# Transposes by the DMA crossbar in a transformer block on one core: LayerNorm output, attention output and phi(k)

## The chip, the core and the metric

The kernel runs on one core of a Trainium2 chip. The metric is the device time of one execution in microseconds. A core has a matrix engine (TensorE, PE in the profile), a vector engine (VectorE, DVE), an engine for activations (ScalarE, ACT), a general one (GpSimd, POOL), a queue engine that only issues transfers (SyncE, SP), and 16 DMA engines. SBUF is the on-chip memory of 128 partitions; PSUM is the small memory into which TensorE writes. Each engine works through its own list of instructions in order, and waits on semaphores for the others.

## The reference

```
x = A_x                                             # 2048 tokens x 448
sa, ca, ga, sb, cb, gb = split(silu(c) @ w_mod)     # six vectors of 448
h = layernorm(x) * (1 + ca) + sa
x = x + ga * A(h)
h = layernorm(x) * (1 + cb) + sb
x = x + gb * B(h)

A: q, k, v = h @ wq, h @ wk, h @ wv                 # 16 heads of 28
   for each of 4 segments of 512 tokens, per head:
       p = softmax(q k^T * 28**-0.5 + causal mask);  a_dot = p v
       a_mem = phi(q) M / (phi(q) z + 1e-6)
       o = g * a_mem + (1 - g) * a_dot              # g = sigmoid(beta)
       M += phi(k)^T v;  z += sum(phi(k))           # phi(t) = t + 1 if t > 0 else exp(t)
   return o @ wo
B: return (sigmoid(h @ w_gate) * (h @ w_up)) @ w_down    # 1792 wide
```

Inputs and outputs are bfloat16.

## The kernel before

The 2048 tokens are four segments of 512, and a segment is four tiles of 128 tokens. The 448 features are cut in four chunks of 112 (`KP`, `NK`). The 16 heads stand in four groups of four (`hc`), each head padded to 32 partitions (`HP`), so that four heads fill the 128 partitions of `qT` and `kT`.

A segment passes through these jobs:

- LayerNorm (class `LN`, lines 206 to 224): statistics, reciprocal root on GpSimd, and `norm`, which writes `xn`, a tile of 128 tokens by 448 features.
- `h_chunk` (line 226): TensorE transposes one chunk of the four `xn` tiles into PSUM (`lntr`), and ScalarE (odd chunks) or VectorE (even ones) scales and shifts it into `hT`, features by tokens. It runs for the first LayerNorm (key `("1", s)`) and the second (`("2", s)`).
- `proj_qk`, `proj_v` (lines 267 to 284): the projections; `qT` and `kT` come out transposed, `vt` not.
- `mem_k` (line 289): `kT` is transposed by TensorE into PSUM (`ptk`), and phi is worked out there by ScalarE and VectorE into `pk`; `mem_update` (line 305) multiplies `pk` with `vt` and adds to the memory `M_sb`.
- `logits` and `pv` (lines 325 and 356), one head group at a time: scores, `exp` on ScalarE, masks on GpSimd; then the products with `vt` and, after segment 0, with the memory. VectorE and GpSimd combine both into `ou`.
- `otr` (line 402): TensorE transposes `ou` into PSUM, VectorE copies it to `oT`. `wo_tile` (line 412) multiplies with `wo`, adds to `x_sb` and begins the second LayerNorm.
- `gate_up` (line 425) and `down` (line 441): the feed-forward part.

The order is written out by hand: a manual schedule in which each engine's list follows the order of the calls. The loop over segments and head groups (from line 551) places `logits`, `pv` and `otr`; between them `run_fill` takes jobs from a list, `fill`, until their listed cost reaches a quota. `fill` holds the projections and memory jobs of the next segment, the output projection and the second LayerNorm of the segment before (appended after that segment's last `otr`), and the feed-forward jobs. `blend` weaves the first LayerNorm of the next segment between those jobs. `later(n, fn)` holds a piece back for n jobs, so that VectorE doesn't stand waiting. PSUM has four buffers (`m`) that projections, transposes and products share, and one large one for the scores.

All transfers run on SP's queue in order, but for three early ones on ScalarE's. The program has eight semaphores for them, used in turn (lanes): a transfer waits until the one eight places before it, on either queue, has landed. `wd_sb` is the landing place of `wq` and `wk` at the start and is loaded with `w_down` later.

Of the kernel before, what the change touches and what calls it, by code (L numbers as in the profile page):

```python
# [17 lines left out]
def kernel(  # L18
# [24 lines left out]
    KP, NK = 112, 4  # L43
    assert KP * NK == D and H * Dh == D and L == 512 and TPS == 4 and F == NFC * P
# [62 lines left out]
    wq_sb = wts.tile([KP, NK, H, HP], BF16)  # L107
    wk_sb = wts.tile([KP, NK, H, HP], BF16)
    wv_sb = wts.tile([KP, NK, D], BF16)
    wo_sb = wts.tile([KP, NK, D], BF16)  # L110
    wg_sb = wts.tile([KP, NK, F], BF16)
    wu_sb = wts.tile([KP, NK, F], BF16)
    wd_sb = wts.tile([P, NFC, D], BF16)
    beta_t = const.tile([P, H], BF16)
    wq_st = wd_sb[0:KP, 0:NK, :].rearrange("p k (h d) -> p k h d", d=Dh)
    wk_st = wd_sb[0:KP, NK:2 * NK, :].rearrange("p k (h d) -> p k h d", d=Dh)
    nc.vector.memset(wq_sb[:, :, :, Dh:HP], 0.0)
    nc.vector.memset(wk_sb[:, :, :, Dh:HP], 0.0)
    nc.sync.dma_start(wq_st, A_wq.rearrange("(k p) (h d) -> p k h d", p=KP, d=Dh))
    nc.scalar.dma_start(wk_st, A_wk.rearrange("(k p) (h d) -> p k h d", p=KP, d=Dh))  # L120
    nc.sync.dma_start(wv_sb[:], A_wv.rearrange("(k p) n -> p k n", p=KP))

    def late_loads():
        load_x(nc.sync, TPS, 2 * TPS)
        nc.sync.dma_start(beta_t[:], A_beta.partition_broadcast(P))
        wm[2] = load_wm(nc.sync, 2)
        load_x(nc.sync, 2 * TPS, 3 * TPS)
        nc.sync.dma_start(wo_sb[:], A_wo.rearrange("(k p) n -> p k n", p=KP))
        wm[3] = load_wm(nc.sync, 3)
        load_x(nc.sync, 3 * TPS, 4 * TPS)  # L130
        for w_sb, w_dram in ((wg_sb, B_w_gate), (wu_sb, B_w_up)):
            wv_ = w_dram.rearrange("(k p) n -> p k n", p=KP)
            nc.sync.dma_start(w_sb[:, 0:2, :], wv_[:, 0:2, :])
            nc.sync.dma_start(w_sb[:, 2:4, :], wv_[:, 2:4, :])
        wm[4] = load_wm(nc.sync, 4)
        nc.sync.dma_start(wd_sb[:], B_w_down.rearrange("(fc p) n -> p fc n", p=P))
        wm[5] = load_wm(nc.sync, 5)
# [10 lines left out]
    cols = const.tile([KP, 4, NK], F32)  # L148
# [12 lines left out]
    vt_all = [const.tile([P, TPS, H, HP], BF16, name=f"vt{s}") for s in range(NSEG)]  # L161
# [18 lines left out]
    def mod_cols(jobs):  # L180
        cp = m_f32("cp")
        for j, vi in jobs:
            for kc in range(NK):
                for k in range(NK):
                    nc.tensor.matmul(cp[0:KP, vi * NK + kc:vi * NK + kc + 1], lhsT=wm[j][:, k, kc * KP:(kc + 1) * KP],
                                     rhs=silu[:, k:k + 1], start=(k == 0), stop=(k == NK - 1))
        for j, vi in jobs:
            src = cp[0:KP, vi * NK:(vi + 1) * NK]
            if vi % 2:
                nc.vector.tensor_scalar(cols[:, vi, :], src, 1.0, None, op0=ALU.add)  # L190
            else:
                nc.vector.tensor_copy(cols[:, vi, :], src)
# [10 lines left out]

    class LN:
        def __init__(self, srcs, key):
            self.srcs, n = srcs, len(srcs)
            self.mv = work.tile([P, n, nc.vector.BN_AGGR_DIM], F32, tag=f"mv{n}", bufs=4, name="mv")
            self.rs = work.tile([P, n], F32, tag=f"rs{n}", bufs=4, name="rs")
            self.out = xns_of.setdefault(key, [])
# [6 lines left out]
        def rstd(self):  # L216
            nc.gpsimd.tensor_scalar(self.rs[:], self.mv[:, :, 1], EPS, None, op0=ALU.add)
            nc.gpsimd.tensor_tensor(self.rs[:], self.rs[:], mhalf[:, 0:len(self.srcs)], ALU.pow)

        def norm(self, i):  # L220
            xn = work.tile([P, D], BF16, tag="xn", bufs=8, name="xn")
            nc.vector.tensor_scalar(xn[:], self.srcs[i], self.mv[:, i, 0:1], self.rs[:, i:i + 1],
                                    op0=ALU.subtract, op1=ALU.mult)
            self.out.append(xn)

    def h_chunk(xns, hT, kc, vi, act_kc=(1, 3)):
        pt = m_bf16("lntr")
        for t in range(TPS):
            nc.tensor.transpose(pt[0:KP, t * P:(t + 1) * P], xns[t][:, kc * KP:(kc + 1) * KP], ident[:])  # L229
        if kc in act_kc:  # L230
            nc.scalar.activation(hT[:, kc, :], pt[0:KP, 0:L], AF.Identity, scale=cols[:, vi + 1, kc:kc + 1],  # L231
                                 bias=cols[:, vi, kc:kc + 1])
        else:
            nc.vector.tensor_scalar(hT[:, kc, :], pt[0:KP, 0:L], cols[:, vi + 1, kc:kc + 1],  # L234
                                    cols[:, vi, kc:kc + 1], op0=ALU.mult, op1=ALU.add)

    xns_of, hT_of = {}, {}

    def ln1_jobs(s):
        box = []  # L240

        def first():
            box.append(LN([x_sb[:, s * TPS + t, :] for t in range(TPS)], s))
            box[0].stats(0)
        jobs = [first] + [lambda t=t: box[0].stats(t) for t in range(1, TPS)] + [lambda: box[0].rstd()]
        jobs += [lambda: None] + [lambda t=t: box[0].norm(t) for t in range(TPS)]
# [10 lines left out]
    def new_hT(key):  # L257
        hT_of[key] = pipe.tile([KP, NK, L], BF16, tag="hT", bufs=3, name="hT")
# [30 lines left out]
    def mem_k(s, t):  # L289
        if t == 0:  # L290
            pk_of[s] = pipe.tile([P, TPS, 512], BF16, tag="pk", bufs=1, name="pk")
        ptk = m_bf16("ptk")
# [315 lines left out]
```

The softmax here doesn't subtract the row's maximum and nothing guards it: scores larger than these inputs give would overflow.

## Time and profile before

| | before |
|---|---|
| median of 3 runs | 307.42 us (307.2 to 311.83) |
| the profiled execution: time | 307.21 us |
| the profiled execution: span, first to last instruction | 305.5 us |
| TensorE busy, matmuls | 277.3 us, 2256 |
| VectorE busy | 175.4 us |
| ScalarE busy | 151.5 us |
| GpSimd busy | 99.6 us |
| mean granted TensorE clock | 0.955 |
| transposes on TensorE: `lntr`, `ptk`, `otr` | 128, 48, 64 |

The profile shows one execution. A group line gives the source line, the engine, the operation, output and inputs with their shapes and the count; then busy time and the mean of one; then the idle time of the engine just before them and what ended it. A line of the windows gives, for a stretch of time, each engine's busy time and count, the granted clock (1.00 is full speed), the share of the DMA engines that is busy, and GB/s. A waits line gives who waited for whom: us in total, how often, and the longest. A line of DMA issues gives the count, the size of each, and the median time from issue to landing. Engines overlap, so shares do not add up to the span.

### The profile page before, as it was taken

How to read it: one execution, taken by the hardware profiler on the slowest of the kernel's cores; microseconds unless marked ns; L12 is line 12 of the kernel's file. 1: busy time of each engine (PE TensorE's matmuls, PEld its weight loads, DVE VectorE, ACT ScalarE, POOL GpSimd, SP SyncE). 2: the span in 40 equal slices, each digit the busy share in tenths (PEclk: the TensorE clock that was granted, in tenths of full speed). 3: DMA queues.
4: the chain of work that ended last, by engine and by line, in shares of the span. 5: the costliest groups of instructions: out<-in, count | busy, mean ns of one | idle time of the engine just before them, and what ended most of it. 6: DMA issues, size and time to landing. Idle time of an engine off the chain costs nothing.

```text
span 305.5 us, 5534 instructions
## 1 busy us (share of the span) xinstructions
PE 277.3 (91%) x2256; PEld 142.9 (47%) x2256; DVE 175.4 (57%) x393; ACT 151.5 (50%) x185; POOL 99.6 (33%) x159
## 2 busy tenths in 40 slices
PE   8888599699886979999998999998999998999995
PEld 3534346284543335545455354444644544544452
DVE  3647694863589535466786254779637558333331
ACT  1456658545955365657436467661675320133300
POOL 0336152713697813131543314326233104000000
PEclk9899999958999689999999799999999999999999
DMA  6999101720000000000001000000100000100001
GB/s 163 280 292 294 58 0 32 233 56 0 3 0 2 0 0 3 0 2 0 2 15 47 0 2 0 4 2 12 35 15 2 0 2 9 37 15 2 0 15 45
DMA packets 12472, 12.84 MB, mean 42 GB/s; under 512 B 1184, under 2 KB 11552, under 8 KB 12448
## 3 DMA queue, kind: packets, MB, share of 16 engines
q1 hardware_dynamic: 11248, 11.48, 13.6%
q10 hardware_dynamic: 1200, 1.03, 1.2%
q8 instruction: 17, 0.28, 0.4%
q14 instruction: 7, 0.06, 0.1%
HBM read 10.67 MB, written 1.84 MB: 41 GB/s over the span
## 4 chain that ended last, share of the span: by engine, by line
PE 66%; DVE 16%; ACT 9%; DMA 3%; issue 3%; POOL 2%; SPq 0%; DVEq 0%; ACTq 0%
PE gps L431 16%; PE ups L436 16%; PE dps L444 13%; PE pq L271 7%; ACT pT L341 5%; PE lg L338 4%; PE acc L366 3%; DMA wd_sb<-in_A_wq_dram 3%; DVE st L213 3%; PE pv L282 2%; DVE x_sb L418 2%; DVE pk L300 2%; DVE pqt L349 2%; ACT hT L231 1%; PE otr L408 1%
## 5 line engine op out<-in xcount | busy, mean ns | idle before, releaser
L341 ACT ACTIVATE pT<-lg 128x2048 bf16<-128x2048 f32 (+1 forms) x48 | 76.5, 1594 | 59.9 <-PE lg L338 59.7
L439 DVE SCALAR_TENSOR_TENSOR fT<-tt,ups 128x512 bf16<-128x512 f32 x56 | 38.4, 686 | 58.2 <-PE ups L436 44.6
L353 POOL TENSOR_SCALAR_AFFINE_SELECT pT<-pT 128x512 bf16<-128x512 bf16 x64 | 40.0, 640 | 68.4 <-ACT pT L341 68.2
L431 PE MATMUL gps<-hT,wg_sb 112*128 112x512 bf16 x224 | 60.1, 389 | 2.0 <-DVE hT L234 0.8
L436 PE MATMUL ups<-hT,wu_sb 112*128 112x512 bf16 x224 | 59.2, 388 | 0.0
L433 ACT ACTIVATE tt<-gps 128x512 f32<-128x512 f32 x56 | 32.9, 596 | 40.4 <-PE gps L431 37.6
L444 PE MATMUL dps<-wd_sb,fT 128*128 128x448 bf16 x224 | 44.2, 353 | 2.3 <-DVE t L393 1.3
L436 PEld LDWEIGHTS <-wu_sb 112*128 112x128 bf16 x224 | 22.0, 100 | 28.7 <-issue 3.3
L431 PEld LDWEIGHTS <-wg_sb 112*128 112x128 bf16 x224 | 20.5, 99 | 27.6 <-issue 5.9
L444 PEld LDWEIGHTS <-fT 128*128 128x128 bf16 x224 | 21.3, 98 | 23.4 <-DVE t L393 1.7
L400 POOL TENSOR_TENSOR ou<-t,t 128x448 bf16<-128x448 f32 x12 | 13.8, 1146 | 53.4 <-DVE t L399 53.4
L271 PE MATMUL pq<-hT,wq_sb 112*128 112x512 bf16 x64 | 19.4, 425 | 5.2 <-DVE pk L300 1.9
L448 DVE TENSOR_TENSOR ot<-dps,x_sb 128x448 bf16<-128x448 f32 x16 | 9.9, 621 | 20.0 <-PE dps L444 20.0
L366 PEld LDWEIGHTS <-pT 128*128 128x128 bf16 x640 | 18.4, 96 | 4.7 <-issue 2.2
L213 DVE BATCH_NORM_STATS2 st<-x_sb 128x6 f32<-128x448 bf16 x32 | 19.8, 618 | 1.1 <-DMA x_sb<-in_A_x_dram 0.6
L271 PE MATMUL pq<-hT,wk_sb 112*128 112x512 bf16 x64 | 19.2, 429 | 0.9 <-DVE x_sb L418 0.9
L366 PE MATMUL acc<-vt,pT 128*128 128x29 bf16 x640 | 18.5, 176 | 1.4 <-DVE pk L300 1.4
L338 PE MATMUL lg<-qT,kT 28*128 28x512 bf16 (+3 forms) x256 | 17.8, 311 | 1.5 <-DVE kT L276 0.8
L231 ACT ACTIVATE hT<-lntr,cols 112x512 bf16<-112x512 bf16 x16 | 11.9, 779 | 14.3 <-PE lntr L229 14.3
L276 DVE CAST kT<-pq 128x512 bf16<-128x512 f32 x16 | 10.9, 679 | 9.8 <-PE pq L271 9.8
L229 PE MATMUL lntr<-ident,xn 128*112 128x128 bf16 x128 | 11.7, 230 | 4.6 <-ACT vt L284 1.8
L274 ACT CAST qT<-pq 128x512 bf16<-128x512 f32 x16 | 9.5, 591 | 12.2 <-PE pq L271 12.1
(78 smaller groups left out, 305.5 us busy)
## 6 DMA issues: line engine op xcount, KB each, us to landing
wm<-in_w_mod_dram SPq DMA_DIRECT2D x5, 392.0 KB, 5.2
out_dram<-ot SPq DMA_DIRECT2D x16, 112.0 KB, 1.7
wg_sb<-in_B_w_gate_dram SPq DMA_DIRECT2D x2, 784.0 KB, 12.4
wu_sb<-in_B_w_up_dram SPq DMA_DIRECT2D x2, 784.0 KB, 15.5
wd_sb<-in_B_w_down_dram SPq DMA_DIRECT2D x1, 1568.0 KB, 8.1
x_sb<-in_A_x_dram SPq DMA_DIRECT2D x3, 448.0 KB, 8.8
wm<-in_w_mod_dram ACTq DMA_DIRECT2D x1, 392.0 KB, 6.1
wd_sb<-in_A_wk_dram ACTq DMA_DIRECT2D x1, 392.0 KB, 8.6
```

The lines of the kernel that those rows point to most:

```text
L213: nc.vector.bn_stats(st[:], self.srcs[i])
L231: nc.scalar.activation(hT[:, kc, :], pt[0:KP, 0:L], AF.Identity, scale=cols[:, vi + 1, kc:kc + 1], bias=cols[:, vi, kc:kc + 1])
L271: nc.tensor.matmul(pq[:, 0:L], lhsT=head_cols(w_sb, k, hc), rhs=h[:, k, :], start=(k == 0), stop=(k == NK - 1))
L338: nc.tensor.matmul(lg[:, hs, wid:wid + nq], lhsT=kT[r, hc, kb * P:(kb + 1) * P], rhs=qT[r, hc, kb * P:L], start=True, stop=True, tile_posi ...
L341: nc.scalar.activation(pT[:, :, w0:w0 + wid], lg[:, :, 0:wid], AF.Exp, scale=scale)
L353: nc.gpsimd.affine_select(out=blk, in_=blk, compare_op=ALU.is_ge, fill=0.0, base=0, pattern=[[0, 4], [1, P]], channel_multiplier=-1)
L366: nc.tensor.matmul(accv[:, qb, hs, 0:ME], lhsT=pT[:, hs, c0:c0 + P], rhs=vt[:, kb, hc * 4 + hs, 0:ME], start=(kb == 0), stop=(kb == qb))
L431: nc.tensor.matmul(gp[:, 0:L], lhsT=wg_sb[:, k, fs], rhs=h[:, k, :], start=(k == 0), stop=(k == NK - 1))
L433: nc.scalar.activation(tt[:], gp[:, 0:L], AF.Tanh, scale=0.5)
L436: nc.tensor.matmul(up[:, 0:L], lhsT=wu_sb[:, k, fs], rhs=h[:, k, :], start=(k == 0), stop=(k == NK - 1))
L439: nc.vector.scalar_tensor_tensor(ft[:], tt[:], 1.0, up[:, 0:L], op0=ALU.add, op1=ALU.mult)
L444: nc.tensor.matmul(dp[:, 0:D], lhsT=fT_of[(s, fc)][:, t * P:(t + 1) * P], rhs=wd_sb[:, fc, :], start=(fc == 0), stop=(fc == NFC - 1))
```

## The change

Three of the four places where TensorE transposes now use a DMA from SBUF to SBUF that transposes (`dma_start_transpose`), all issued on SP's queue: the normalized tiles (for the second LayerNorm, and for the first from segment 1 on; segment 0's first LayerNorm keeps TensorE, as `pe_chunk`), the attention output, and phi(k). Each moves 128 partitions by 512 columns. The feature chunks become 128 rows, the last of them half zeros (`LW` is 64), so `xn` is 512 columns wide with zeros behind the 448; `ou` is padded to 32 columns for each head, and the rows of `wo` are spread out to match. Scale and shift are done on `hT` in place, by VectorE alone. phi(k) is worked out on `kT` before the transpose. The weight loads change shape with the chunks, the loads of the feed-forward weights move from SP's queue to ScalarE's, and the jobs are woven in a different order.

```diff
-    wq_sb = wts.tile([KP, NK, H, HP], BF16)
+    wq_sb = wts.tile([P, NK, H, HP], BF16)
...
+    def load_w(eng, dst, w):
+        eng.dma_start(dst[:, 0:3, :], w[0:3 * P, :].rearrange("(k p) n -> p k n", p=P))
+        eng.dma_start(dst[0:LW, 3, :], w[3 * P:D, :])
...
     def late_loads():
...
-        nc.sync.dma_start(wo_sb[:], A_wo.rearrange("(k p) n -> p k n", p=KP))
+        nc.gpsimd.memset(wo_sb[:], 0.0)
+        for hs in range(4):
+            nc.sync.dma_start(wo_sb[HP * hs:HP * hs + Dh, :, :],
+                              A_wo.rearrange("(c h d) n -> h d c n", h=4, d=Dh)[hs])
...
+        nc.gpsimd.memset(wg_sb[LW:P, 3, :], 0.0)
+        nc.gpsimd.memset(wu_sb[LW:P, 3, :], 0.0)
+
+    def ffn_load_jobs():
+        jobs = []
+        for w_sb, w in ((wg_sb, B_w_gate), (wu_sb, B_w_up)):
+            for k in range(0, 3):
+                jobs.append((0, lambda w_sb=w_sb, w=w, k=k: nc.scalar.dma_start(w_sb[:, k, :], w[k * P:(k + 1) * P, :])))
+            jobs.append((0, lambda w_sb=w_sb, w=w: nc.scalar.dma_start(w_sb[0:LW, 3, :], w[3 * P:D, :])))
+        jobs.append((0, lambda: nc.scalar.dma_start(wd_sb[:], B_w_down.rearrange("(fc p) n -> p fc n", p=P))))
+        return jobs
...
+        def norm_t(self, i):
+            self.norm(i)
+            if i == 0:
+                self.h = new_hT(self.key)
+            nc.sync.dma_start_transpose(self.h[:, :, i * P:(i + 1) * P], self.xn[:, i, :])
+
+        def modulate(self, kc, vi):
+            h = self.h[:, kc, :]
+            nc.vector.tensor_scalar(h, h, cols[:, vi + 1, kc:kc + 1], cols[:, vi, kc:kc + 1],
+                                    op0=ALU.mult, op1=ALU.add)
...
-        jobs = [first] + [lambda t=t: box[0].stats(t) for t in range(1, TPS)] + [lambda: box[0].rstd()]
-        jobs += [lambda: None] + [lambda t=t: box[0].norm(t) for t in range(TPS)]
+        nop = lambda: None
+        jobs = [first] + [lambda t=t: box[0].stats(t) for t in range(1, TPS)]
+        jobs += [lambda: box[0].rstd(0, TPS), nop] + [lambda t=t: box[0].norm_t(t) for t in range(TPS)]
+        jobs += [nop, nop, nop] + [lambda kc=kc: box[0].modulate(kc, 0) for kc in range(NK)]
...
-        ptk = m_bf16("ptk")
-        for hc in range(NHC):
-            nc.tensor.transpose(ptk[:, hc * P:(hc + 1) * P], kT_of[s][:, hc, t * P:(t + 1) * P], ident[:])
-        ek = work.tile([P, 512], BF16, tag="e", bufs=3)
-        nc.scalar.activation(ek[:], ptk[:, 0:512], AF.Exp)
...
+    def mem_k(s, hc):
+        if hc == 0:
+            pk_of[s] = pipe.tile([P, NHC, TPS, P], BF16, tag="pk", bufs=1, name="pk")
+        pkt = work.tile([P, L], BF16, tag="pqt", bufs=3, name="pkt")
+        pk = pk_of[s]
+        phi(kT_of[s][:, hc, :], pkt[:], 2, lambda: nc.sync.dma_start_transpose(pk[:, hc, :, :], pkt[:]))
...
-        op = m_bf16("otr")
-        for t in range(TPS):
-            nc.tensor.transpose(op[0:KP, t * P:(t + 1) * P], ou[:, t, :, :].rearrange("p h d -> p (h d)"), ident[:])
-        nc.vector.tensor_copy(oT_of[s][:, hc, :], op[0:KP, 0:L])
+        nc.sync.dma_start_transpose(oT_of[s][:, hc, :, :], ou[:].rearrange("p t h e -> p (t h e)"))
...
-        ln = LN([xt], ("2", s))
-        ln.stats(0)
-        ln.rstd()
-        later(2, lambda: ln.norm(0))
+        ln.stats(t)
+        ln.rstd(t, t + 1)
+        later(2, lambda: ln.norm_t(t))
...
     def prep_b1():
         ga = mod_rep(2, 1.0, "ga")
+        wm[4] = load_wm(nc.sync, 4)
...
-    fill.extend(blend(j0[7:9] + late + j0[9:], ln1_jobs(1), 2))
-    j1 = j1[:5] + m[0][0:2] + j1[5:7] + m[0][2:4] + j1[7:9] + m[0][4:] + j1[9:] + [(1000, prep_b1)]
-    fill.extend(blend(j1, ln1_jobs(2), 5))
-    j2 = j2[:5] + m[1][0:2] + j2[5:7] + m[1][2:4] + j2[7:9] + [(2000, prep_b2)] + m[1][4:] + j2[9:]
-    fill.extend(blend(j2, ln1_jobs(3), 5))
-    fill.append((1000, prep_b3))
-    fill.extend(j3[:5] + m[2][0:2] + j3[5:7] + m[2][2:4] + j3[7:9] + m[2][4:] + j3[9:])
+    fill.extend(blend(blend(j0[2:4] + [(0, late_consts)] + j0[4:] + m[0][0:4], ln1_jobs(1), 1), ffn_load_jobs(), 3, 2))
+    fill.extend(blend(j1[:6] + m[0][4:] + j1[6:] + m[1][0:4] + [(1000, prep_b1)], ln1_jobs(2)))
+    fill.extend(blend(j2[:6] + m[1][4:] + [(2000, prep_b2)] + j2[6:] + m[2][0:4] + [(1000, prep_b3)], ln1_jobs(3)))
+    fill.extend(j3[:6] + m[2][4:] + j3[6:])
```

The jobs of transposes, of phi(k) and of modulation now have a listed cost of 0 in `fill`. The new `phi` helper does for k what `logits` did for q: `exp` on ScalarE, and a minimum and a combining instruction on VectorE, held back two jobs.

## The prediction

> **What bounds the kernel now.** I read the busy table first, then the time slices, then the stages in windows, then TensorE's waits, then the groups and the DMA issues.
>
> ```profile
> PE 277.3 (91%) x2256; PEld 142.9 (47%) x2256; DVE 175.4 (57%) x393; ACT 151.5 (50%) x185; POOL 99.6 (33%) x159
> PEclk9899999958999689999999799999999999999999
> ```
>
> TensorE is the only engine near full, so work taken off it should shorten the span. But the average hides stages, and the clock row falls to 5, 6 and 7 in single slices. The windows cut the span at four events: the first query projection (13.5), the first projections of segment 1 (33.5), the first output projection (90.8) and the first gate projection (111.8).
>
> ```profile
> 13.50:33.50 20.00, 16.41 (x100) 7.30 (x99) 10.71 (x24) 14.27 (x20) 8.33 (x20) 0.94 0.99 270
> 33.50:90.80 57.30, 49.16 (x510) 29.20 (x509) 37.84 (x83) 35.78 (x49) 27.33 (x35) 0.91 0.16 44
> 90.80:111.80 21.00, 16.25 (x128) 7.94 (x127) 14.30 (x33) 11.91 (x14) 14.01 (x20) 0.83 0.00 1
> 111.80:305.50 193.70, 184.62 (x1452) 92.45 (x1452) 105.92 (x233) 86.29 (x101) 46.89 (x74) 0.98 0.03 11
> ```
>
> The columns are TensorE, weight loads, VectorE, ScalarE and GpSimd, then the granted clock and the DMA share. The last stage is TensorE at 95% and full clock. The three before are 77 to 86% busy with the clock at 0.83 to 0.94: there TensorE waits for others, and after a wait it runs slowly (62.0 to 70.7 us stand at a clock of 0.50 throughout). The waits of 27 to 112 us say for whom:
>
> ```profile
> PE pq L271 <- DVE pk L300: 1.9, 2, 1.6
> ...
> PE lntr L229 <- ACT vt L284: 1.8, 2, 1.4
> PE pq L271 <- ACT hT L231: 1.6, 2, 1.3
> PE acc L366 <- DVE pk L300: 1.4, 1, 1.4
> ```
>
> Most end in results of the three transposes (`pk`, `hT`) that the change moves.
>
> **What leaves TensorE.** 112 of 128 `lntr`, all 48 `ptk`, all 64 `otr`.
>
> ```profile
> L229 PE MATMUL lntr<-ident,xn 128*112 128x128 bf16 x128 | 11.7, 230 | 4.6 <-ACT vt L284 1.8 <-DVE xn L222 0.9 <-DVE t L399 0.8
> ...
> L408 PE MATMUL otr<-ident,ou 128*112 128x128 bf16 x64 | 6.3, 220 | 0.7 <-ACT qT L274 0.7
> ...
> L294 PE MATMUL ptk<-ident,kT 128*128 128x128 bf16 x48 | 4.2, 219 | 1.9 <-DVE ou L390 1.0 <-DVE pk L300 0.6 <-ACT qT L274 0.2
> ```
>
> Busy time includes each batch's drain under the next one, so I price from start to next start in the timeline: four `lntr` 30.26 to 30.53 (68 ns each), eight `ptk` 30.53 to 30.97 (55 ns), four `otr` 45.09 to 45.41 (80 ns). That is 7.6 + 2.6 + 5.1 = 15.3 us of TensorE in all. ScalarE loses 14 evictions of 0.78 us (L231), VectorE 14 of 0.54 (L234) and 16 of 0.42 (L409); it gains 28 in-place modulations, priced at the normalization's 0.42 us (L222: same operation, SBUF to SBUF, 448 columns). TensorE's other matmuls keep their count and width; 128 rows in place of 112 change nothing, since L436 (112 rows, 512 columns) and L510 (128 rows) both step by 0.21 to 0.22 us at full clock.
>
> **What comes in: 56 DMA transposes of 128x512, all on SP's queue.** No row shows one. Let T be the time from the source's last write to landing. Lower bound: the nearest row by size, direction and quiet rings, the output stores, at 1.7 us; upper bound: a 448 KB load among others, 8.8 us.
>
> ```profile
> out_dram<-ot SPq DMA_DIRECT2D x16, 112.0 KB, 1.7
> ...
> x_sb<-in_A_x_dram SPq DMA_DIRECT2D x3, 448.0 KB, 8.8
> ...
> x_sb<-in_A_x_dram SPq DMA_DIRECT2D x1, 224.0 KB, 4.8
> ```
>
> I stay near the store: 1.7 x 128/112 = 1.9, plus half a microsecond to issue (SP's loads: 0.3 to 0.8), so T = 2.5 us in quiet rings. Up to 34 us the rings are full (DMA share 0.99), and I take the 224 KB row's 4.5.
>
> The store row prices a copy, not a transpose. The Trainium skill (VectorE: DVE Perf Modes, The three transpose paths) gives 1309 ns for a 128x128 block through the DMA crossbar against 390 ns on TensorE, and advises TensorE where PSUM will do. If four blocks followed one another, T would be about 5.2 us, an estimate from that page, and the sum below would end near 303.
>
> **Stage by stage.**
>
> 0 to 13.5: nothing. The first LayerNorm keeps TensorE's transposes. The weight loads become pairs, and SP waits for earlier landings between them; the chain was `wq`'s landing at 11.7, and less is queued ahead of it. Gain or loss under 1 us.
>
> 13.5 to 33.5: a loss of 5. Three memsets of 1792 columns now run on GpSimd before its first mask, by `bmask` (464 columns, 0.80 us) about 3.1 us each, from 11.6 to 20.9, where the mask began at 20.07: everything behind moves 0.9. Segment 1's last `xn` ended at 29.2; now 30.1, plus T = 4.5 gives 34.6. VectorE is then held in order at the first modulation, and two `phi` pairs (0.29 + 0.75) stand between the four modulations: 4 x 0.42 + 2 x 1.04 = 3.8, so 38.4 where the last chunk was consumed at 33.1. Nothing covers it but one block of logits. ScalarE meanwhile issues nine weight loads (0.5 us each by its own rows), and the ninth, `wd`, waits for the first transpose on its semaphore lane; behind it stand the last `vt` eviction and the `phi` exponentials, which wait for the same hand-over. If TensorE did not wait there, this would cost about 3 us by itself.
>
> 33.5 to 111.8: a gain of 11. Removed here: 32 `lntr`, 40 `ptk`, 16 `otr`: 2.2 + 2.2 + 1.3 = 5.7. The waits on `pk` and around `ptk` and `lntr` total about 6; I take half, 3, since `phi` stays on ScalarE and VectorE. The slow clock of 62.0 to 70.7 cost 4.3; it follows 2.9 us of idle that `pk` made; half, 2. Segments 2 and 3 have three value projections and `rp`, `acc`, `lg` (5 us) between the last normalization and the first use, so T + 0.42 is hidden; their cover fails from T of about 4.5. The attention transposes start as soon as `ou` is written, some 6 us ahead of the output projection. Then the order changes: four `pq` and one `pv` that stood behind the first output projection now stand ahead of it (+4.3 there, -4.3 behind). Behind it, 21.0 us become the chain: evacuation 0.7, VectorE's list from the first residual add to the last normalization 11.3 (91.5 to 102.8, as now), T = 2.5, four modulations 1.7: 16.2, against 7.7 of matmuls that cover it. Sum: -5.7 - 3 - 2 + 4.3 - 4.8 = -11.2.
>
> 111.8 to 305.5: a gain of 4. Removed: 48 `lntr` (3.3), 44 `otr` (3.5), waits of `lntr` on `t` and of `gps` on `hT` (1.8). Against it: at the last three hand-overs the transposes have 8 to 14 us of down projections over them, but the modulations stand on VectorE behind the last output add: 0.62 + 4 x 0.42, less 0.3 of logits and TensorE's own pace, 1.5 each. -8.6 + 4.5 = -4.1.
>
> Sum: 305.5 + 5 - 11.2 - 4.1 = 295.2 us of span. The profiled execution took 307.21, 1.7 more than its span, and the median is 0.2 above that: 297 us.
>
> **Rivals.**
> - Early stages give nothing (A). For it: VectorE is 66% and ScalarE 62% busy from 33.5 to 90.8, and `phi`, exponentials and casts stay; the waits may only change names. Against it: the waits end in `pk` and `hT`. Then stages two to four return only what the order returns, about 5 for the 5 lost, and the last stage's 4.1 is offset by the ScalarE delay of 3: 306.
> - T is long (B), the one that ends slower. One transpose holds SP's queue until it is nearly done, and every one behind it is late. Price: each us of T above 2.5 costs 1 at the first gate hand-over and, above 4.5, 1 at segments 1, 2 and 3 each; above 6 also 1 at three output projections. T = 6 gives 297 + 3.5 + 4.5 = 305, T = 7.2 is 2% slower, 8.8 gives about 325. For it: four transposes come 0.4 to 0.8 us apart in segment 1. Against it: the store row, and 128 KB is little beside the 270 GB/s of the first stages.
> - All hidden (C): T is 1.9, the first stage loses 2 in place of 5, and the whole slow clock and all waits on `pk` come back: 297 - 3 - 5 = 289.
> - That the transposes are not moved can be excluded: the built program has 56 on SP's queue and 224 matmuls fewer on TensorE.
>
> **How the numbers follow.** Forecast 0.55 (own range 290 to 302), A 0.22, B 0.15, C 0.08. Faster by over 2%, below 301.3, which is about what a measurement of this kernel can tell from no change: 0.52 of the forecast and C, 0.60. Within 2%: A and the forecast's edge, 0.25. Slower: 0.15, B beyond 7.2. The range runs from just under C (286) to 310, B at T of about 6.7; what lies above is most of B, below little.
>
> **What would show it.** In the profile after: transposes landing 2 to 3 us after issue; a TensorE gap of some 8 us around 30 to 38; no stretch at clock 0.5 near 62 to 70; first gate projection at about 106 to 107; the last stage 4 us shorter. The forecast is wrong if SP's queue shows transposes waiting for one another, if the gap before the first gate projection exceeds 12 us, or if TensorE's idle time in 33 to 111 stays as it was.

## The result, and the profile after

The changed kernel takes 323.74 us (median of 4 runs, 322.88 to 324.93), the kernel before 309.52 beside it (307.2 to 311.83): a ratio of 1.049 with a 95% interval of 1.037 to 1.060. It is slower. Ratios are of the means of undisturbed executions: a few executions (one of the four of before here, two of the four of e11 below) ran in a slower state, at a lower clock, and are left out of the ratios. The forecast was 297, with a range of 286 to 310; it missed by 27 us. The profiled execution took 324.38 us, with a span of 322.4.

The busy table and the clock row of the page of the changed kernel:

```profile
PE 267.0 (83%) x2032; PEld 126.3 (39%) x2032; DVE 184.2 (57%) x403; ACT 141.7 (44%) x171; POOL 105.9 (33%) x162
PEclk9969657989999957999679799999968999999999
```

TensorE has 224 matmuls and 10 us of busy time less, as meant. But its share fell from 91 to 83%, and single slices of the clock row still stand at 5, 6 and 7, now far into the last stage too. The windows say where. They are cut at the same events in both kernels: the first query projection, the end of segment 1's first projection, the first gate projection, and the end of the run. (The 33.5 us of the prediction is the end of that projection, not its beginning, as the lines of before further down show.)

```profile
18.20:48.20 30.00, 15.34 (x72) 5.53 (x71) 14.95 (x35) 12.12 (x19) 7.67 (x19) 0.73 0.85 221
48.20:117.30 69.10, 53.73 (x529) 26.99 (x526) 49.17 (x106) 41.72 (x51) 39.36 (x51) 0.92 0.30 62
117.30:322.40 205.10, 186.66 (x1364) 87.99 (x1364) 107.68 (x232) 83.80 (x96) 50.87 (x79) 0.93 0.10 25
```

Against before (13.5, then 20.0, 78.3 and 193.7 us), with what was forecast for each:

| stage | before, us | after, us | change | forecast |
|---|---|---|---|---|
| to the first query projection | 13.5 | 18.2 | +4.7 | 0 |
| to the end of segment 1's first projection | 20.0 | 30.0 | +10.0 | +5 |
| to the first gate | 78.3 | 69.1 | -9.2 | -11.2 |
| to the end | 193.7 | 205.1 | +11.4 | -4.1 |
| span | 305.5 | 322.4 | +16.9 | -10.3 |

In the last stage TensorE has 88 matmuls fewer (1364 for 1452) and is busy 2 us longer (186.66 for 184.62): the clock fell from 0.98 to 0.93. The rest is waiting, and TensorE's waits over the whole span name one producer above all, the in-place modulation of transposed LayerNorm output (line L261):

```profile
PE pq L312 <- DVE hT L261: 18.8, 8, 11.8
PE gps L471 <- DVE hT L261: 14.1, 8, 5.3
PE lg L383 <- ACT pT L386: 4.2, 3, 2.0
```

The columns are microseconds in all, times, and the longest. Most landings are as fast as assumed. The DMA issues, with the median from issue to landing last:

```profile
hT<-xn SPq DMA_TRANSPOSE x28, 2.3
...
oT<-ou SPq DMA_TRANSPOSE x16, 2.4
...
pk<-pkt SPq DMA_TRANSPOSE x12, 2.5
```

T was forecast at 2.5 us in quiet rings, and there the time of one transpose is not what was wrong. At segment 1's hand-over, beside weight loads, it was. First before, where TensorE has three of the four matmuls of that projection done early and waits 1.3 us for the last:

```profile
30.97 0.81 PE L271 MATMUL pq<-hT,wq_sb 112*128 112x512 bf16 x3
33.08 0.38 PE L271 MATMUL pq<-hT,wq_sb 112*128 112x512 bf16 x1 [1.30 <-ACT hT L231]
```

The same place in the changed kernel; the last line is the time from issue to landing of these four transposes:

```profile
32.59 1.61 DVE L250 TENSOR_SCALAR xn<-x_sb,mv,rs 128x448 bf16<-128x448 bf16 x4 [1.99 <-POOL rs L247]
33.32 5.36 SPq L257 DMA_TRANSPOSE hT<-xn  x4
43.78 0.41 DVE L261 TENSOR_SCALAR hT<-hT,cols 128x512 bf16<-128x512 bf16 x1 [2.65 <-DMA hT<-xn]
44.25 0.61 PE L312 MATMUL pq<-hT,wq_sb 128*128 128x512 bf16 x1 [11.76 <-DVE hT L261]
...
47.15 1.01 PE L312 MATMUL pq<-hT,wq_sb 128*128 128x512 bf16 x2 [0.93 <-DVE hT L261]
DMA to landing us min/median/max: 2.5/3.4/6.2
```

The last tile was written at 34.2 and VectorE could begin at 43.8: by the prediction's own definition (from the source's last write to landing) T was 9.5 us there.

### The profile page after: what moved, and what is told of

Its sections match the earlier page's. It is cut to its first block, busy times and chain, and to the rows that moved or that the text cites. A ratio compares the mean times of both kernels' runs of the same rounds, so it can differ in the third digit from the quotient of the medians.

```text
span 322.4 us, 5232 instructions
## 1 busy us (share of the span) xinstructions
PE 267.0 (83%) x2032; PEld 126.3 (39%) x2032; DVE 184.2 (57%) x403; ACT 141.7 (44%) x171; POOL 105.9 (33%) x162
## 4 chain that ended last, share of the span: by engine, by line
PE 52%; DVE 23%; DMA 9%; ACT 6%; POOL 5%; issue 3%; SPq 1%; POOLq 0%; ACTq 0%; DVEq 0%
PE gps L471 14%; PE ups L476 14%; PE dps L484 11%; ACT pT L386 5%; DMA hT<-xn 5%; PE pq L312 4%; DVE xn L250 4%; DVE hT L261 3%; PE acc L405 3%; DVE st L242 3%; PE lg L383 3%; PE pwo L453 3%; DMA pk<-pkt 2%; DVE e L335 2%; DVE pkt L336 2%
## 5 line engine op out<-in xcount | busy, mean ns | idle before, releaser
L471 PE MATMUL gps<-hT,wg_sb 128*128 128x512 bf16 x224 | 63.5, 400 | 14.9 <-DVE hT L261 14.1
L476 PE MATMUL ups<-hT,wu_sb 128*128 128x512 bf16 x224 | 60.3, 393 | 0.0
L471 PEld LDWEIGHTS <-wg_sb 128*128 128x128 bf16 x224 | 20.8, 100 | 43.9 <-issue 17.1
L312 PE MATMUL pq<-hT,wq_sb 128*128 128x512 bf16 x64 | 20.8, 437 | 18.8 <-DVE hT L261 18.8
L476 PEld LDWEIGHTS <-wu_sb 128*128 128x128 bf16 x224 | 22.5, 101 | 29.8 <-issue 5.4
L261 DVE TENSOR_SCALAR hT<-hT,cols 128x512 bf16<-128x512 bf16 x28 | 14.5, 564 | 12.6 <-DMA hT<-xn 12.6
L250 DVE TENSOR_SCALAR xn<-x_sb,mv,rs 128x448 bf16<-128x448 bf16 x32 | 16.8, 545 | 6.5 <-POOL rs L247 6.5
L312 PE MATMUL pq<-hT,wk_sb 128*128 128x512 bf16 x64 | 19.3, 430 | 0.9 <-DVE kT L317 0.9
L541 POOL TENSOR_TENSOR wd_sb<-wd_sb,gb 128x448 bf16<-128x448 bf16 x14 | 15.4, 1111 | 6.4 <-ACT gb L225 6.4
L453 PE MATMUL pwo<-wo_sb,oT 128*128 128x448 bf16 x64 | 16.1, 409 | 0.9 <-DMA oT<-ou 0.8
```

Of the source, the lines that this page charges most:

```text
L250: nc.vector.tensor_scalar(self.xn[:, i, 0:D], self.srcs[i], self.mv[:, i, 0:1], self.rs[:, i:i + 1], op0=ALU.subtract, op1=ALU.mult)
L312: nc.tensor.matmul(pq[:, 0:L], lhsT=head_cols(w_sb, k, hc), rhs=h[:, k, :], start=(k == 0), stop=(k == NK - 1))
L471: nc.tensor.matmul(gp[:, 0:L], lhsT=wg_sb[:, k, fs], rhs=h[:, k, :], start=(k == 0), stop=(k == NK - 1))
L476: nc.tensor.matmul(up[:, 0:L], lhsT=wu_sb[:, k, fs], rhs=h[:, k, :], start=(k == 0), stop=(k == NK - 1))
```

## Experiments

Theory 1 was that the transposes on the crossbar expose idle time at every LayerNorm hand-over, and a slow TensorE clock behind it. Theory 2 was that the edits beside them cost (memsets on GpSimd, weight loads on ScalarE's queue, listed costs of 0, the new order of jobs). Ratios are to the kernel before, run beside each; its median lay between 307.4 and 309.5 us on these occasions, so small steps between kernels that did not run side by side are uncertain by about 2 us. Windows, waits and timelines are of one execution each.

**e1: the memsets run early.**

```
+    nc.gpsimd.memset(wo_sb[:], 0.0)             # behind mhalf's memset
+    nc.gpsimd.memset(wg_sb[LW:P, 3, :], 0.0)
+    nc.gpsimd.memset(wu_sb[LW:P, 3, :], 0.0)
-    ... the same three in late_loads()
```

> Edit: the three GpSimd memsets (padding of the output projection, the gate and the up weights) run before the first LayerNorm instead of beside it. Everything else is as in the changed kernel. Theory 2 (side edits): the memsets share something with VectorE; with them gone from 11.6 to 16.6 us the first four normalizations (L250) fall from 4.5 back to about 1.8 us in all, the first projection starts near 13.6 instead of 18.2, and the whole is 4 to 5 us shorter, near 319. Rival: the slow normalizations have another cause (the transposes' buffers, the wider rows), the start stays at 18 and the time at 324.

Measured: 320.77 us, ratio 1.043 (1.036 to 1.050), and the first projection at 14.3 us. The timeline of the changed kernel, GpSimd first, then VectorE (start, duration, then engine, line and tiles):

```profile
11.61 1.71 POOL L137 MEMSET wo_sb<- 128x1792 bf16 x1
13.38 1.60 POOL L143 MEMSET wg_sb<- 64x1792 bf16 x1
14.92 1.72 POOL L144 MEMSET wu_sb<- 64x1792 bf16 x1
...
10.63 4.47 DVE L250 TENSOR_SCALAR xn<-x_sb,mv,rs 128x448 bf16<-128x448 bf16 x4 [1.49 <-POOL rs L247]
```

and VectorE's same four normalizations with the memsets out of the way (e1):

```profile
10.84 1.77 DVE L250 TENSOR_SCALAR xn<-x_sb,mv,rs 128x448 bf16<-128x448 bf16 x4 [1.57 <-POOL rs L247]
```

4.47 us against 1.77, with nothing changed but what GpSimd does meanwhile. The longest of the normalizations takes 1.74 us, about one memset. So the start is settled: 3.9 of the 4.7 us come back there, and 3.0 reach the end by the medians (the intervals overlap). From e4 to e5 below, the same edit is worth 4.4 us by the ratios. All later kernels with "early memsets" have this edit.

**e2, e3, e4: loads back on SyncE; LayerNorm on TensorE; everything on TensorE.**

```
e2:  -  nc.scalar.dma_start(w_sb[:, k, :], ...), nc.scalar.dma_start(wd_sb[:], ...)
     +  nc.sync.dma_start(...), in late_loads() and, for wd_sb, in prep_b1()
e3:  -  ln.norm_t(t) ... [(0, ... modulate(kc, 2))]
     +  ln.norm(t)   ... [(4 * TR, ... pe_chunk(kc, 2))], and the same in ln1_jobs()
e4:  e3, and phi(k) and otr() as in the kernel before (16 transposes and 4 in PSUM)
```

> Edit: the gate and up weights are loaded on SyncE's queue behind the last rows of x, and the down weights on SyncE in front of the fifth modulation matrix, as the kernel before had them; ScalarE issues no load inside the stages. The transposes stay on the crossbar. Theory 2 (side edits): the 11.8 us that TensorE waits near 32 to 44 us are made by loads that fill the rings while the transposes are under way, and by ScalarE's queue standing 5 us at the down weights; the gap falls to about 6 (four transposes of 1.2 us in a row and 2.3 us of landing), and the time by 6 to 8 us to about 317. Theory 1 (the transposes themselves): the gap stays over 10 us and the time falls by less than 2.

> Edit: the 128 transposes of LayerNorm output go back to TensorE (four to a PSUM tile, the modulation in the eviction, half of it on ScalarE), with the cost that the planner had for them before; phi(k) and attention output stay on the crossbar. Theory 1 (the transposes themselves): every hand-over behind a LayerNorm shortens; the gaps of 11.8, 3.8, 2.9, 6.2 us and those of the second halves go, less 8.7 us of transposes (128 at 68 ns) that TensorE does again, and the time falls by 15 to 20 us, to about 306. Theory 2 (side edits): most of the loss stays, since loads, memsets and job order are unchanged: 318 to 324.

> Edit: all three groups of transposes (LayerNorm output, phi(k), attention output) go back to TensorE; what is left of the change is the 128-row chunks with padding, the memsets, the loads on ScalarE's queue and the new order of jobs. Theory 1 (the transposes themselves): the rest costs about the 4.7 us of the start, so near 311; above the LayerNorm-only variant if the crossbar pays for phi(k) and attention output, below it if it does not: 96 transposes less are 5.7 us (32 at 80 ns and 64 at 55 ns are 6.1). Theory 2 (side edits): 320 or more, the transposes off TensorE being worth what they were forecast to be and the rest eating it.

Measured: e2 323.76 us, ratio 1.051 (1.043 to 1.058); e3 309.98, 1.006 (1.002 to 1.011); e4 309.39, 1.001 (0.996 to 1.005).

In e2 the gate and up weights load earlier and the down weights later. The four transposes of segment 1 land faster, and the 11.8 us wait falls to 7.7:

```profile
DMA to landing us min/median/max: 2.3/2.4/2.4
40.23 0.61 PE L314 MATMUL pq<-hT,wq_sb 128*128 128x512 bf16 x1 [7.66 <-DVE hT L263]
```

So some 4 us of that wait are the loads beside the transposes. But the whole gained nothing: the 1568 KB load then ran beside segment 1's phi(k) transposes, and TensorE waited 4.4 us for them at 77 us. Neither theory had that. e3 says that the LayerNorm transposes hold most of the loss (some 14 us of it), as theory 1 had it. e4 says that the side edits together cost nothing, although the memsets among them cost 3. So something among them had to be a gain.

**e5 and e6: all on TensorE with early memsets; attention output alone on the crossbar.**

```
e5:  e4 with the memsets of e1
e6:  e5, but otr() keeps  nc.sync.dma_start_transpose(oT_of[s][:, hc, :, :], ...)
```

> Edit: all three groups of transposes on TensorE (309.4 us as measured) and the three GpSimd memsets moved ahead of the first LayerNorm. What remains of the change is the 128-row chunks, the loads and the job order. Theory 2 (side edits hold one loss, the memset clash, and one gain, the new order of jobs): the start falls from 18.5 to 14.5 us and the whole by 3 to 4 us, to about 305.5, faster than the kernel before. Rival: the start is given back at the first hand-over to segment 1, and the time stays at 309.

> Edit: as the previous kernel (memsets early, LayerNorm and phi(k) transposes on TensorE), but the attention output goes through the crossbar: 64 transposes off TensorE (5.1 us by the forecast's 80 ns each), and off VectorE the 16 copies out of PSUM. Theory 1: the crossbar costs where its landing is waited for; here two blocks of work lie between issue and use in most blocks, so 3 to 5 us less than the all-TensorE kernel with early memsets, about 301 to 302. Rival: what is gained is lost again at the output projections (waits of 0.8 to 1.7 us each, seen twice) and through longer busy queues: equal to it within 1 us.

Measured: e5 303.36 us, ratio 0.986 (0.978 to 0.995); e6 301.41, 0.980 (0.973 to 0.986). What remains of the change without any DMA transpose (128-row chunks, loads, a new order of jobs; not separated further) is worth 1.4%, about 4 us. The attention output by DMA is worth about 2 more by the medians (the intervals overlap), where 64 transposes had been priced at 5.1 us. Both kernels beat the kernel before.

**e7: matmuls that nobody reads, in the gaps.**

```
+    def idle_mm(n):
+        dm = m_f32("dmy")
+        for _ in range(n):
+            nc.tensor.matmul(dm[:], lhsT=ident[:], rhs=..., start=True, stop=True)   # 512 columns
     h2_jobs:   + [(0, lambda: idle_mm(16 if s < 3 else 1))]
     proj_jobs: + [(0, lambda: idle_mm(32 if s == 1 else 12))]   # segments 1 to 3
```

> Edit: the changed kernel with matmuls of 512 columns whose result nobody reads, placed on TensorE in front of the first gate projections of segments 0 to 2 (16 each) and of the first projections of segments 1 (32), 2 and 3 (12 each): 104 in all, 22 us of work at full clock, into gaps where TensorE waits for landed and modulated LayerNorm output. Theory 1a (most of the loss is the half clock after the gaps, not the gaps): the clock rises from 0.91 to 0.95 or more and the time falls by 5 to 9 us although 104 matmuls are added. Theory 1b (the gaps themselves): the clock behind a gap does not matter, the time is unchanged, or up to 5 us longer where the added matmuls overrun a gap.

Measured: 320.63 us, ratio 1.040 (1.028 to 1.051); the clock rose from 0.91 to 0.95. About 22 us of useless work were added and the kernel became 3 us shorter by the medians (the intervals overlap). Its last stage in the windows:

```profile
118.50:316.20 197.70, 185.40 (x1398) 89.34 (x1396) 106.87 (x232) 83.72 (x96) 48.92 (x77) 0.98 0.10 26
```

197.7 us instead of 205.1, with 34 matmuls more. They do not make the modulated rows earlier: at the first hand-over of this stage the gate's first four matmuls end 5.6 us behind the logits ahead of them (177.4 to 183.1 in the changed kernel), and 5.7 here (174.4 to 180.1). What they change is the clock, 0.98 in this stage instead of 0.93. So a gap costs its own length and then a stretch at half clock.

**e8: the listed costs as before.**

```
-    [(0, ... modulate(kc, 2))]   [(0, ... mem_k(s, hc))]
+    [(4 * TR, ...)]              [(4 * TR, ...)]          # and ln1_jobs' modulations
```

> Edit: the changed kernel, where the planner's listed cost of a modulation and of a phi(k) job is 240 again and not 0, so that each softmax block takes the quota of filling work that it had before. No instruction is added or removed, only their order. Theory 2 (the filling work runs out before the second segment's last blocks): the three logits in a row and the 4.2 us that TensorE waits for the exponentials vanish, and 3 to 4 us with them, to about 320. Rival: the quota is not what empties the list; unchanged at 324 within 1 us.

Measured: 320.62 us, ratio 1.043 (1.035 to 1.050). The last stage shortened to 196.3 us and TensorE's waits for exponentials from 4.2 to 2.2, but the first gate moved from 117.3 to 122.3. It is 3 us less than the changed kernel, with intervals that overlap: order matters, but this was a shift more than a cure.

**e9 and e10: where the modulations run, and when.** Both start from e1.

```
e9:   if kc % 2: nc.scalar.activation(h, h, AF.Identity, scale=..., bias=...)
      else:      nc.vector.tensor_scalar(h, h, ...)
e10:  - fill.extend(down_jobs(s - 2)); fill.extend(h2_jobs(s - 1) + gu_jobs(s - 1))
      + dn = down_jobs(s - 2) if s >= 2 else []
      + fill.extend(dn[:3] + h2_jobs(s - 1) + dn[3:] + gu_jobs(s - 1))
```

> Edit: as the changed kernel with early memsets (320.8 us as measured), all transposes on the crossbar, but of the four modulations at a hand-over the odd ones run on ScalarE, as half of the evictions did before. Theory 1c (one engine in order is the cost): at the first gate projection four modulations take 3.5 us in a row on VectorE behind the landing; split, each hand-over shortens by 1 to 1.5 us, so 4 to 7 us over six. Rival: what counts is the landing and the first modulation, and ScalarE's are longer and stand behind exponentials; the time stays within 2 us.

> Edit: as the changed kernel with early memsets (320.8 us), but the modulations of segments 1 and 2 are put in front of the last of the four down projections that fill the hand-over, not behind it. Theory 1d (the landing is long past there, only VectorE's order is late): the waits of 3.5 and 3.3 us for the modulated rows in the last stage go, with the half clock of some 5 to 10 us behind each, and the time falls by 5 to 9 us. Rival: the landed rows themselves are late; at most 1 us.

Measured: e9 315.68 us, ratio 1.026 (1.019 to 1.033), 5 less than e1. e10 309.06, ratio 1.003 (0.999 to 1.008), 12 less than e1, from the place of four modulations in two segments. This hand-over in the changed kernel, SyncE's queue, then VectorE, then TensorE:

```profile
164.34 4.57 SPq L257 DMA_TRANSPOSE hT<-xn  x3
...
169.63 1.19 SPq L257 DMA_TRANSPOSE hT<-xn  x1
...
177.55 0.62 DVE L488 TENSOR_TENSOR ot<-dps,x_sb 128x448 bf16<-128x448 f32 x1 [2.35 <-PE dps L484]
178.09 0.40 DVE L261 TENSOR_SCALAR hT<-hT,cols 128x512 bf16<-128x512 bf16 x1
180.38 0.29 DVE L335 TENSOR_SCALAR e<-e 128x512 bf16<-128x512 bf16 x1 [1.88 <-ACT e L332]
180.71 0.69 DVE L336 SCALAR_TENSOR_TENSOR pqt<-qT,e 128x512 bf16<-128x512 bf16 x1
181.32 1.05 DVE L261 TENSOR_SCALAR hT<-hT,cols 128x512 bf16<-128x512 bf16 x3
...
181.78 1.30 PE L471 MATMUL gps<-hT,wg_sb 128*128 128x512 bf16 x3 [2.85 <-DVE hT L261]
```

The issue of the last transpose began at 169.63, and the landing takes 2.3 us from there: the rows were there at about 172. VectorE idled 2.35 us before 177.55 with that work ready, because in its order the last output add stood in front, and that waited for the last down projection. After one modulation the order put a phi(q) pair in front of the other three, and that waited 1.88 us for ScalarE. TensorE stood meanwhile. The same place in e10, VectorE and then TensorE:

```profile
173.11 2.05 DVE L261 TENSOR_SCALAR hT<-hT,cols 128x512 bf16<-128x512 bf16 x4
175.54 0.62 DVE L488 TENSOR_TENSOR ot<-dps,x_sb 128x448 bf16<-128x448 f32 x1 [0.38 <-PE dps L484]
...
175.77 1.04 PE L471 MATMUL gps<-hT,wg_sb 128*128 128x512 bf16 x4
```

No wait is left, and e10's last stage takes 193.9 us where e1's takes 205.2. The same 1364 matmuls are busy 182.1 us in e10 and 186.7 in the changed kernel: some 4.5 of the 11 us are clock, the rest idle time.

**e11 and e12: which LayerNorm.**

```
e11:  e1, second LayerNorm (wo_tile, h2_jobs) by norm() and pe_chunk()
e12:  e1, both by norm() and pe_chunk()
```

> Edit: early memsets, and of the LayerNorm transposes only the second LayerNorm's (in front of the gate projections) go back to TensorE; the first LayerNorm's (in front of the projections) stay on the crossbar, as do phi(k) and attention output. Read with the next kernel it splits the cost of the LayerNorm transposes. Theory 1: the second LayerNorm holds most, since its chain runs from the output projection to the gate without other work between; 11 to 13 us go, so 308 to 310. Rival: the gap of 11 us at segment 1's projections is the larger part: over 314.

> Edit: early memsets, all LayerNorm transposes on TensorE, phi(k) and attention output on the crossbar. Against the kernel with the attention output alone on the crossbar (301.4 us) this prices phi(k) by DMA; against the changed kernel with early memsets (320.8) all of LayerNorm by DMA. Theory 1: phi(k) is wanted one segment late and hides: 300 to 303. Rival: phi(k) costs, since four of its transposes hold the queue for 5 to 8 us while attention outputs stand behind them: 304 to 307.

Measured: e11 314.86 us (median of 310.81, 313.89, 315.83 and 317.78; no interval), e12 304.84, ratio 0.990 (0.984 to 0.996). With e6 and e1 this is a ladder, each step with one group more on the crossbar; for e11 it has the mean of the first two executions:

| on the crossbar, early memsets | us | step |
|---|---|---|
| nothing (e5) | 303.4 | |
| attention output (e6) | 301.4 | -2.0 |
| and phi(k) (e12) | 304.8 | +3.4 |
| and first LayerNorm (e11) | 312.4 | +7.5 |
| and second LayerNorm (e1) | 320.8 | +8.4 |

phi(k) costs: e12 has a wait that is not in e6.

```profile
PE dM L355 <- DMA pk<-pkt: 5.0, 3, 2.8
```

The two LayerNorms cost about the same. Which costs more is not shown, since the two executions of e11 are 3 us apart; the 11 to 13 us expected of the second did not come. And the second one's step hangs on the order: with the modulations of e10 in place, the crossbar (309.1) is no longer behind TensorE (310.8 and 313.9) for it; the profiled last stages take 193.9 and 197.1 us.

**e13, e14, e15: the first LayerNorm.** All start from e10.

```
e13:  m[s][0:4] (the phi(k) jobs) from behind segment s's jobs to behind j{s+1}[:2]
e14:  e13, wd_sb's load by SyncE in prep_b2() instead of ScalarE in segment 0
e15:  e13, run_fill((quota if s else 0.8 * quota) + debt)
```

> Edit: early memsets, modulations ahead of the last down projection (309.1 us as measured), and the four phi(k) jobs of each segment moved behind the modulations and the first two projections of the next one, so that nothing of phi(k) stands in front of a modulation on VectorE. Order theory: in the kernel it starts from, the modulations of segment 1 are done at 45.2 us, of which 4.4 is one phi(k) product waiting for a free buffer and some 5 are waits and work for its exponentials; the gaps of 10.9 + 0.6 + 4.4 us shrink to 6 to 8 in all and the time falls by 7 to 10 us, to about 300. Landing theory: the four transposes and the full rings set the gap; less than 3 us.

> Edit: as the kernel before in this list, and the 1568 KB load of the down weights moves from ScalarE's queue in segment 0 to SyncE's queue behind the sixth modulation matrix, some 50 us later. Collision theory: the transposes of segment 1 land in 2.5 us instead of 4 to 6, ScalarE does not stand 5 us behind a semaphore lane; 2 to 4 us less than the kernel before in this list. Rival: the collision moves with the load, to the transposes that run beside it at 85 to 95 us; no change or 1 to 3 us longer.

> Edit: as the first kernel of this list, and segment 0's softmax blocks take 0.8 of the quota of filling work, so that more projections are left when the first output projection is reached and stand between it and the first gate. Cover theory: the first gate's gap of 5.3 us closes, with the half clock behind it; 3 to 6 us less than the first kernel. Rival: segment 0's blocks then lack filling work and wait for their exponentials instead; within 1 us or longer.

Measured: e13 321.04 us, ratio 1.040 (1.031 to 1.049); e14 319.15, 1.035 (1.028 to 1.042); e15 318.19, 1.031 (1.022 to 1.040). All are some 8 to 11 us slower than e10 by the ratios.

The reading of the hand-over was right in part. In e10, ScalarE (first line) and VectorE stand like this:

```profile
35.33 0.53 ACT L325 CAST vt<-pv 128x448 bf16<-128x448 f32 x1 [5.09 <-DMA hT<-xn]
...
36.42 0.29 DVE L335 TENSOR_SCALAR e<-e 128x512 bf16<-128x512 bf16 x1 [6.89 <-ACT e L332]
...
43.87 0.69 DVE L336 SCALAR_TENSOR_TENSOR pkt<-kT,e 128x512 bf16<-128x512 bf16 x1 [3.71 <-DMA pk<-pkt]
44.48 0.73 DVE L261 TENSOR_SCALAR hT<-hT,cols 128x512 bf16<-128x512 bf16 x2
```

ScalarE's eviction stands behind the load of the down weights, which waits for a transpose; the exponentials behind it are late; VectorE waits for them with modulations queued behind; and the fourth phi(k) waits until a transpose frees a buffer, with the last two modulations behind it. In e13 the three gaps of 10.9, 0.6 and 4.35 us became one of 8.7, close to the expected 6 to 8. What is left of it is the landing:

```profile
36.08 1.38 DVE L261 TENSOR_SCALAR hT<-hT,cols 128x512 bf16<-128x512 bf16 x4 [6.50 <-DMA hT<-xn]
```

But the phi(k) transposes now had too little work over them, and the wait came back under another name (e13, 44 to 110 us):

```profile
PE dM L356 <- DMA pk<-pkt: 11.5, 7, 2.4
```

with the clock at 0.66 to 0.87 in the windows from 30 to 90 us. The first gate came at 124.9 instead of 115.0. In e14 the DMA share from 30 to 45 us fell from 0.76 to 0.30, and the gap stayed (9.4 us): the load of the down weights is not what makes it. That does not clear the loads as a whole: beside the gate and up weights the four transposes still landed 4.0 to 6.0 us after issue, where e2's took 2.3 to 2.4. In e15 the first gate's gap shrank from 5.3 to 3.8, but an attention output written at 88.5 us was transposed only at 102.1, since SyncE's queue had four phi(k) transposes in front that waited for their sources; the output projection waited 10.7 us for it.

**e16: on the crossbar only what has cover.**

```
e6 with e10's order, and of the second LayerNorm:
+    later(2, lambda: (ln.norm_t if s in (1, 2) else ln.norm)(t))
+    if s in (1, 2): return [(0, ... modulate(kc, 2))]
```

> Edit: early memsets; on the crossbar only attention output and the second LayerNorm of segments 1 and 2 (modulated ahead of the last down projection); phi(k), the first LayerNorms and the second of segments 0 and 3 on TensorE. By the account so far the crossbar pays where other matmuls lie between landing and use: 301.4 us less 32 transposes at 68 ns (2.2 us) and a little clock, 297 to 300. If the gain seen from the order of the modulations was only the undoing of a self-made wait, no better than 301.4.

Measured: 300.75 us, ratio 0.974 (0.965 to 0.982). It beats both kernels and stands beside e6 (0.973 to 0.986): the profiled last stage is 4 us shorter (189.0 for 193.4), but the medians do not tell the two apart.

## Why the prediction was wrong

By size, the miss of 27 us is the last stage (15.5), segment 1's hand-over (5.0), the start (4.7) and the way to the first gate (2.0).

- **The last stage: forecast -4.1, measured +11.4.** The place was right: "the modulations stand on VectorE behind the last output add". The term was mis-sized: 1.5 us for each of three hand-overs. By e1 and e10, two of them cost 11.7 us together. The working counted the add and four modulations. It left out what else stands on VectorE there (at the first hand-over the phi(q) pair and its wait for ScalarE) and the slow clock after the gap; e7 shows the last by itself. The third hand-over, where no such work stands, has a wait of 1.1 us, close to its 1.5. The gain of 8.6 us did not come either: with both hand-overs mended, e10's last stage takes 193.9 us where before took 193.7. TensorE is busy 182.1 us there for 184.6, at a clock of 0.95 for 0.98, and 4.2 us of waits for exponentials are new. Why the clock stays lower there is not shown.
- **Segment 1's hand-over: forecast +5, measured +10.0.** The parts named were the right ones, and all but one had the right size: the last tile at 34.2 (forecast 30.1, and the start is 4.7 late), 3.6 us from the first modulation to the end of the fourth (forecast 3.8). The term that failed is T, 9.5 us for 4.5: three transposes stand ahead of the last one on SyncE's queue, 1.2 to 1.3 us each, and the last one landed 6.2 us after its issue began at 37.5. In e2, without loads beside them, the landings take 2.3 to 2.4 us and the wait is 4.1 us shorter.
- **The start: forecast nothing, measured +4.7.** The memsets were priced on GpSimd's own list only. They took 1.6 to 1.7 us, not 3.1; what they did to VectorE was not in the sum. e1 shows it. The Trainium skill (SBUF — State Buffer, Who interferes with whom) states that the two engines share a pair of ports as an exclusive lock, taken for a whole instruction by VectorE's `tensor_scalar` in its two-port modes or by a GpSimd instruction. The trace agrees: the two long normalizations (1.73 and 1.74 us) begin within 0.1 us of the memsets of 1.71 and 1.60 us.
- **To the first gate: forecast -11.2, measured -9.2.** The chain behind the first output projection was sized well: 102.4 to 117.3 is 14.9 us for a forecast of 16.2, although the gate starts after one modulation and the fourth ends at 119.9. What failed is "so T + 0.42 is hidden" for segments 2 and 3: TensorE waited 3.8 and 1.6 us. In segment 2 the landings take 2.3 us, but the four transposes are issued over 5.1 us and two phi(k) pairs stand between the modulations. In segment 3, beside a load of `w_mod`, the landings take 3.8 to 4.6 us. And up to 52 us the clock is 0.5.
- **What leaves TensorE: 15.3 us.** The ladder never shows it. Of 5.1 us of attention output about 2 arrived. A likely reason, not tested by itself, is that a transpose which TensorE ran inside a wait for something else was free.
- **A term that was not in the sum at all:** what the chunks, loads and job order gain without the transposes, about 4 us (e5, ratio 0.986). It hides part of what the crossbar costs, which from e5 to e1 is 17 us.
- **Rival B** ("every one behind it is late") was given 0.15. Its mechanism is seen at segment 1, where T was 9.5 us. By its own prices that is 5 us there; at the other hand-overs T was 2.4 to 4.6, nearly free by the same prices. That its far end, T = 8.8 everywhere and 325 us, is near the measured 323.7 is luck: most of the loss came from the order on VectorE, the clock and the memsets, which it does not have. (At the 5.2 us taken from the page its prices also give 302, not the 303 of the prediction.)

Open: how the 7.5 us of the first LayerNorm divide between the four issues in series, the loads beside them and the order on VectorE. e13 changed both the order and the cover of phi(k), so it does not settle that.

## What to carry to other kernels

Price a moved transpose not by its own latency but by what stands around its two ends: the queue that issues it in order, the loads that run beside it, and the in-order engine that works on the landed data. Put that work at the first place where the data can have landed and not at the place where it is consumed; on VectorE, four instructions moved by one job at each of two hand-overs were worth 12 us here. Move only what has other TensorE work over it (the attention output was, by about 2 us), and count for each remaining gap the half clock behind it as well.

## What the runs showed of the hardware

- A 128x512 transpose from SBUF to SBUF holds SyncE's queue for 1.19 us and, with little else moving, lands 2.3 to 2.5 us after issue; beside loads it took up to 6.2 (segment 1). Four in a row take 5.1 to 5.4 us to issue. The Trainium skill (VectorE: DVE Perf Modes, The three transpose paths) has 1309 ns for a 128x128 block; an estimate of four such blocks, 5.2 us, is too long for one of these transposes in quiet rings.
- VectorE is slow beside GpSimd at other places too, though no run changes GpSimd's work there. At the first gate the four modulations take 3.55 us, while products of 1.0 us and masks run on GpSimd; the single one at 178.09 above, beside none, takes 0.40:

```profile
114.86 1.02 POOL L541 TENSOR_TENSOR wd_sb<-wd_sb,gb 128x448 bf16<-128x448 bf16 x1
...
117.03 2.10 POOL L541 TENSOR_TENSOR wd_sb<-wd_sb,gb 128x448 bf16<-128x448 bf16 x2
...
116.37 3.55 DVE L261 TENSOR_SCALAR hT<-hT,cols 128x512 bf16<-128x512 bf16 x4 [2.45 <-DMA hT<-xn]
```

- After the gap at segment 1 the clock stayed at 0.5 until 52 us, although TensorE was busy throughout from 48 (windows of the changed kernel; the clock is the third column from the right):

```profile
48.00:50.00 2.00, 2.00 (x9) 0.65 (x9) 0.86 (x3) 1.80 (x2) 0.00 (x0) 0.50 0.32 64
50.00:52.00 2.00, 2.00 (x6) 0.65 (x5) 1.40 (x4) 0.63 (x1) 0.63 (x1) 0.50 0.00 0
52.00:54.00 2.00, 2.00 (x41) 1.34 (x40) 1.39 (x4) 0.58 (x1) 0.00 (x0) 0.88 0.00 0
```

Waits of 0.71 and 2.85 us with one matmul between them were enough to bring the half clock back: from 182 to 184 us 0.54 was granted, and 1.00 again from 186.
